# Attention over 128 heads on one core: unrolled engine programs become loops, and the order of the odd halves changes

## The chip, the cores and the metric

The kernel runs on one core of a Trainium2 chip. The time is the device time in microseconds (us); before the change the median of three runs is 635.95 us (635.76 to 636.34). Lower is better. The engines are TensorE (PE), VectorE (DVE), ScalarE (ACT), GpSimd (POOL) and SyncE (SP); SP and ACT issue the transfers (DMA), which run on 16 DMA engines.

## The reference

```
B, H, Sq, Skv, Dh = 8, 16, 16, 2048, 256          # all bf16
scale  = Dh ** -0.5
scores = einsum('bhqd,bhkd->bhqk', q, k) * scale
attn   = softmax(scores, axis=-1)
out    = einsum('bhqk,bhkd->bhqd', attn, v)
```

There are 128 heads with 16 query rows each. K and V have 134 MB each and are read once; Q and the output have 1 MB each.

## The kernel before, in words

The work is cut into 16 rounds g of 8 heads, and each round into two halves e of 4 heads, here called the even (e = 0, or a) and the odd (e = 1, or b) half. One half of K or V is a unit of 4 MiB: 128 partitions, each with 64 tokens of one head (32 partitions a head), 256 numbers a token. `SL` holds four units: KA, KB, VA, VB. The first K units go to VA and VB, so that the K units of round 1 can follow at once.

For each round:

- DVE transposes K in place, in blocks of 32 by 32 and as 32-bit words (four instructions a unit, line 154), and adds one to `c_kt` after each.
- PE multiplies by the queries (lines 234 and 235). `QW` holds Q spread out with zeros so that one product of 128 rows serves 4 heads; 16 products for half a unit, 64 for a round, into the four banks of `S_ps`. After a half is done, `c_qk` goes up, and SP may reuse the K slot.
- DVE takes the row maximum (line 156), ACT the exponential into `P_sb` with the row sums (line 206), DVE transposes it into `PTc` (line 162), and ACT spreads it by eight copies into `PTz` (line 219, four for each half).
- PE multiplies with V, 64 products for each half (line 251). This is done one round late: in the loop's pass g PE first does the score products of round g and then the output products of round g - 1, both halves.
- ACT reads each half out of `O_ps`, divided by the row sum (line 180), and stores 64 KB a round (line 184). It also writes the next round's queries into `QW` (line 174).

Only PE has a loop (line 266), over the rounds 1 to 15; the programs of SP, DVE and ACT are written out for all rounds. In PE's program the last output products, for round 15, stand behind the loop.

SP issues the loads in a fixed order, and each waits there for its slot: Q, K0a, K0b, K1a, K1b, V0a, V0b, and then for each further round K(g)a, K(g)b, V(g-1)a, V(g-1)b. Nothing behind a waiting load is issued. The last V units go to the K slots, and the very last one comes in eight pieces of 19 to 2 tokens, so that the products can follow the landings.

Of the kernel before, what the change touches and what calls it, by code (L numbers as in the profile page):

```python
# [4 lines left out]
ACTF = mybir.ActivationFunctionType  # L5
ALU = mybir.AluOpType
AX = mybir.AxisListType
PE = mybir.EngineType.PE
BF16 = mybir.dt.bfloat16
F32 = mybir.dt.float32  # L10

T = 64
KA, KB, VA, VB = 0, 1, 2, 3


def bass_standalone__softmax_full_bidir__sampling_kernel(
# [17 lines left out]
    qh = q.rearrange("b h s d -> (b h) (s d)")  # L34
    oh = out.rearrange("b h s d -> (b h s) d")

    with ExitStack() as es:
# [5 lines left out]
        PTc = ec(nc.sbuf_tensor("PTc", [128, T, 32], BF16))  # L43
        PTz = ec(nc.sbuf_tensor("PTz", [128, 2, T, 128], BF16))
        O_fin = ec(nc.sbuf_tensor("O_fin", [128, 2, D], BF16))
        negm = ec(nc.sbuf_tensor("negm", [128, G], F32))
        lsum = ec(nc.sbuf_tensor("lsum", [128, G, 2], F32))
        ltot = ec(nc.sbuf_tensor("ltot", [128, G], F32))
        rinv = ec(nc.sbuf_tensor("rinv", [128, G], F32))

        S_ps = ec(nc.psum_tensor("S_ps", [128, 4, 512], F32))
        O_ps = ec(nc.psum_tensor("O_ps", [128, 4, 512], F32))
# [4 lines left out]
        s_q = sem("s_q")  # L57
        s_k = [sem("s_ka"), sem("s_kb")]
        s_k0 = [sem("s_k0a"), sem("s_k0b")]
        s_v = [sem("s_va"), sem("s_vb")]  # L60
        s_st = [sem("s_st%d" % i) for i in range(2)]
# [4 lines left out]
        c_kt = [[sem("c_kt%d%d" % (e, h)) for h in range(2)] for e in range(2)]  # L66
        c_qk = [sem("c_qka"), sem("c_qkb")]
# [5 lines left out]
        c_pv = [sem("c_pv0"), sem("c_pv1")]  # L73
        c_pl = sem("c_pl")
# [4 lines left out]
        def ap_of(t_ap, offset, dims):  # L79
            return bass.AP(tensor=t_ap.tensor, offset=offset, ap=[list(t_ap.ap[0])] + [list(d) for d in dims])  # L80


        TAIL = [(0, 19), (19, 14), (33, 10), (43, 7), (50, 5), (55, 4), (59, 3), (62, 2)]
        TAIL_A = [(0, 37), (37, 27)]
        s_tail = [sem("s_t%d" % i) for i in range(len(TAIL))]
        s_vl = [sem("s_vl%d" % i) for i in range(len(TAIL_A))]
        s_vc = sem("s_vc")
        s_kl = sem("s_kl")

        def obank(g, e):  # L90
            return e + (2 if g == last else 0)

        def kslot(g, e):
            return (VA, VB)[e] if g == 0 else (KA, KB)[e]
# [3 lines left out]

        def on_sync(eng):
            eng.dma_start(QT[:], qh).then_inc(s_q, 16)  # L100
            for e in range(2):
                load(eng, ku, 0, e, kslot(0, e), 0, T, s_k0[e])
            for g in range(1, G):
                for e in range(2):
                    if g >= 2:
                        eng.wait_ge(c_qk[e], g)
                    if (g, e) != (last, 1):
                        load(eng, ku, g, e, kslot(g, e), 0, T, s_k[e])
                    else:
                        load(eng, ku, g, e, kslot(g, e), 0, 32, s_k[e])  # L110
                        load(eng, ku, g, e, kslot(g, e), 32, 32, s_kl)
                w = g - 1
                for e in range(2):
                    if w:
                        eng.wait_ge(c_pv[e], w)
                    else:
                        eng.wait_ge(c_qk[e], 1)
                    if (w, e) != (last - 1, 1):
                        load(eng, vu, w, e, (VA, VB)[e], 0, T, s_v[e])
                        if e:  # L120
                            eng.sem_inc(s_vc, 16)
                    else:
                        load(eng, vu, w, e, VB, 0, 32, s_v[e])
                        load(eng, vu, w, e, VB, 32, 32, s_vc)

            eng.wait_ge(c_qk[0], G)
            for (a, n), s in zip(TAIL_A, s_vl):
                load(eng, vu, last, 0, KA, a, n, s)
            eng.wait_ge(c_qk[1], G)
            for (a, n), s in zip(TAIL, s_tail):  # L130
                load(eng, vu, last, 1, KB, a, n, s)
            eng.wait_ge(c_ev, 2 * last + 2)
            eng.dma_start(oh[128 * last:128 * last + 128, :], O_fin[:, last % 2, :]).then_inc(s_fin, 16)
            eng.wait_ge(s_fin, 16)

        def on_gpsimd(eng):
            eng.memset(PTz[:].rearrange("p a t c -> p (a t c)").bitcast(F32), 0.0).then_inc(c_pool, 1)  # L137

        def on_vector(eng):
            eng.memset(QW[:].rearrange("p e m x -> p (e m x)").bitcast(F32), 0.0).then_inc(c_qt, 1)  # L140
            eng.wait_ge(s_q, 16)
            qf = QT[:].bitcast(F32)
            eng.transpose(qf, qf).then_inc(c_qt, 1)  # L143
            for g in range(G):
                for e in range(2):
                    for c in range(4):
                        if g == 0 and c == 0:
                            eng.wait_ge(s_k0[e], 16)
                        elif c == 0:
                            eng.wait_ge(s_k[e], 16 * g)  # L150
                        elif (g, e, c) == (last, 1, 2):
                            eng.wait_ge(s_kl, 16)
                        x = SLf[:, kslot(g, e), 16 * c:16 * c + 16, :].rearrange("p t i -> p (t i)")
                        eng.transpose(x, x).then_inc(c_kt[e][c // 2], 1)  # L154
                eng.wait_ge(c_qk[1], g + 1)
                eng.tensor_reduce(out=negm[:, g:g + 1], in_=S_ps[:].rearrange("p c n -> p (c n)"),  # L156
                                  axis=AX.X, op=ALU.max, negate=True).then_inc(c_mx, 1)
                for h in range(2):
                    eng.wait_ge(c_ex[h], g + 1)
                    if g and h == 0:  # L160
                        eng.wait_ge(c_cp, 8 * g)
                    eng.transpose(PTc[:, 32 * h:32 * h + 32, :].rearrange("p t x -> p (t x)"),  # L162
                                  P_sb[:, 1024 * h:1024 * h + 1024]).then_inc(c_pt, 1)
                eng.tensor_reduce(out=ltot[:, g:g + 1], in_=lsum[:, g, :], axis=AX.X, op=ALU.add).then_inc(c_ri, 1)  # L164
                eng.wait_ge(c_ri, 2 * g + 1)
                eng.reciprocal(rinv[:, g:g + 1], ltot[:, g:g + 1]).then_inc(c_ri, 1)  # L166

        def on_scalar(eng):
            def qwb(g):
                Q, r = g // 4, g % 4  # L170
                for a in range(4):
                    dv = QW[32 * a:32 * a + 32, 0, 16 * a, :]
                    sv = QT[32 * Q:32 * Q + 32, :]
                    eng.activation(ap_of(dv, dv.offset, [[1024 + 512, 2], [2, 64], [1, 2]]),  # L174
                                   ap_of(sv, sv.offset + 2 * (8 * r + a), [[8, 2], [64, 64], [1, 2]]),
                                   ACTF.Copy, scale=scale).then_inc(c_qw, 1)

            def evac(g, e):
                rows = slice(64 * e, 64 * e + 64)
                eng.activation(O_fin[rows, g % 2, :], O_ps[rows, obank(g, e), 0:D],  # L180
                               ACTF.Copy, scale=rinv[rows, g:g + 1]).then_inc(c_ev, 1)

            def store(g):
                eng.dma_start(oh[128 * g:128 * g + 128, :], O_fin[:, g % 2, :]).then_inc(s_st[g % 2], 16)

            def finish(g):
                eng.wait_ge(c_ri, 2 * g + 2)
                if g >= 2:
                    eng.wait_ge(s_st[g % 2], 16 * (g // 2))
                for e in range(2):  # L190
                    eng.wait_ge(c_pv[e], g + 1)
                    evac(g, e)
                eng.wait_ge(c_ev, 2 * g + 2)
                store(g)
# [3 lines left out]
            for g in range(G):  # L198
                if g < last:
                    eng.wait_ge(c_qk[1], g + 1)  # L200
                    qwb(g + 1)
                eng.wait_ge(c_mx, g + 1)
                if g:
                    eng.wait_ge(c_pt, 2 * g)
                for h in range(2):
                    eng.activation(P_sb[:, 1024 * h:1024 * h + 1024],  # L206
                                   S_ps[:, 2 * h:2 * h + 2, :].rearrange("p c n -> p (c n)"), ACTF.Exp,
                                   bias=negm[:, g:g + 1], scale=1.0, accum_out=lsum[:, g, h:h + 1]).then_inc(c_ex[h], 1)
                if 0 < g < last:
                    finish(g - 1)  # L210
                if g == 0:
                    eng.wait_ge(c_pool, 1)
                eng.wait_ge(c_pt, 2 * g + 2)
                z = 1 if g == last else 0
                for e in range(2):
                    for a in range(4):
                        rs = 32 * (2 * e + a // 2)
                        sv = PTc[rs:rs + 32, :, :]
# [99 lines left out]
```

## Time and profile before

| what | us |
|---|---|
| median of three runs | 635.95 |
| profiled execution: its own time | 636.1 |
| its span, first to last instruction | 634.8 |
| PE busy (products) | 488.3 |
| DVE busy | 365.2 |
| ACT busy | 214.8 |
| DVE waiting for K to land | 157.9 |
| all transfers | 270.64 MB, mean 426 GB/s |

The span was cut into 40 equal slices; a digit is the busy share of a slice in tenths. The chain of waits goes back from the last instruction to what released it, step by step. In the timeline a row has the start, the duration, the engine, the line, the operation and its operands, and in brackets how long the engine was idle before it and what ended that. Rows of SPq are the moments at which SP issues transfers. A row of a window has the busy time of PE, weight loads, DVE, ACT and POOL, the granted clock of TensorE, the share of the DMA engines and their rate in GB/s.

### The profile page before, as it was taken

Reading aid. Unit: us, or ns where it says so; the run is one execution under the profiler, and the core shown is the slowest. Engines: PE = TensorE matmul, PEld = TensorE weight load, DVE = VectorE, ACT = ScalarE, POOL = GpSimd, SP = SyncE. Lnnn points to the kernel's source line nnn. Section 1 sums busy time; section 2 is a strip of 40 time slices with the busy share of each in tenths; the row PEclk is TensorE's granted clock in tenths of the full one; section 3 lists DMA queues with packets and bytes.
Section 4 is the critical chain, followed back from the end, with each engine's and each line's share of the span. In section 5 each row is a group of like instructions: output and inputs, shape, how many; then the busy total and the mean of one; then the engine's idle time right before and its main releaser. Section 6 shows DMA issues by size and latency. Waiting matters only on the chain.

```text
span 634.8 us, 6396 instructions
## 1 busy us (share of the span) xinstructions
PE 488.3 (77%) x3072; PEld 274.9 (43%) x2560; DVE 365.2 (58%) x210; ACT 214.8 (34%) x289; POOL 7.1 (1%) x5
## 2 busy tenths in 40 slices
PE   0738989595896958869597795967959689595998
PEld 0202828154271532716336262452724527144287
DVE  2968583763738546294562945739366393663830
ACT  1042252525035250342513325142252322524170
POOL 4000000000000000000000000000000000000000
PEclk9978999798997989969799797998979989798899
DMA  8999999999999999999999999999999999999997
GB/s 376 436 441 432 428 432 432 430 430 431 432 429 434 429 432 433 429 434 429 433 430 429 432 429 433 430 430 433 434 429 436 433 433 432 432 432 425 430 425 285
DMA packets 13113, 270.64 MB, mean 426 GB/s; under 512 B 1456, under 2 KB 3760, under 8 KB 4400
## 3 DMA queue, kind: packets, MB, share of 16 engines
q1 hardware_dynamic: 10944, 269.55, 98.8%
q10 hardware_dynamic: 2160, 0.98, 0.5%
q8 instruction: 3, 0.05, 0.0%
q14 instruction: 6, 0.05, 0.0%
HBM read 269.48 MB, written 1.05 MB: 426 GB/s over the span
## 4 chain that ended last, share of the span: by engine, by line
DMA 58%; PE 23%; DVE 16%; ACT 2%; issue 0%; SPq 0%
DMA SL<-in_k_dram 58%; DVE SL L154 15%; PE S_ps L234 11%; PE S_ps L235 10%; PE O_ps L251 2%; ACT PTz L219 1%; DVE PTc L162 1%; DVE negm L156 1%; ACT P_sb L206 0%; ACT O_fin L180 0%; SPq L97 0%; SPq L100 0%; DVE rinv L166 0%; DVE ltot L164 0%
## 5 line engine op out<-in xcount | busy, mean ns | idle before, releaser
L154 DVE STREAM_TRANSPOSE SL<-SL 128x2048 f32<-128x2048 f32 x128 | 284.2, 2279 | 157.9 <-DMA SL<-in_k_dram 157.9
L234 PE MATMUL S_ps<-SL,QW 128*128 128x512 bf16 x512 | 214.0, 418 | 143.5 <-DVE SL L154 143.3
L251 PE MATMUL O_ps<-SL,PTz 128*128 128x256 bf16 x2048 | 226.3, 273 | 0.9 <-ACT PTz L219 0.7
L234 PEld LDWEIGHTS S_ps<-SL,QW 128*128 128x128 bf16 x512 | 75.1, 147 | 326.6 <-issue 171.7
L251 PEld LDWEIGHTS O_ps<-SL,PTz 128*128 128x128 bf16 x2048 | 199.8, 98 | 30.9 <-issue 4.5
L235 PE MATMUL S_ps<-SL,QW 128*128 128x512 bf16 x512 | 212.5, 415 | 0.0
L219 ACT ACTIVATE PTz<-PTc 32x1024 bf16<-32x1024 bf16 x128 | 134.9, 1054 | 11.3 <-ACT O_fin L180 5.9
L174 ACT ACTIVATE QW<-QT 32x256 bf16<-32x256 bf16 x64 | 26.8, 419 | 243.3 <-PE S_ps L235 236.2
L156 DVE TENSOR_REDUCE negm<-S_ps 128x1 f32<-128x2048 f32 x16 | 36.7, 2292 | 61.4 <-PE S_ps L235 61.4
L180 ACT ACTIVATE O_fin<-O_ps,rinv 64x256 bf16<-64x256 f32 x32 | 15.0, 468 | 137.6 <-PE O_ps L251 137.5
L162 DVE STREAM_TRANSPOSE PTc<-P_sb 128x1024 bf16<-128x1024 bf16 x32 | 37.9, 1224 | 20.3 <-ACT P_sb L206 20.3
L206 ACT ACTIVATE P_sb<-S_ps,negm 128x1024 bf16<-128x1024 f32 x32 | 35.3, 1109 | 25.5 <-DVE negm L156 25.5
L137 POOL MEMSET PTz<- 128x8192 f32 x1 | 6.9, 6924 | 0.3 <-POOLq L303 0.3
L206 ACT ACTIVATION_READ_ACCUMULATOR P_sb<-S_ps,negm 128x1 f32 x32 | 6.3, 196 | 0.0
L143 DVE STREAM_TRANSPOSE QT<-QT 128x2048 f32<-128x2048 f32 x1 | 2.3, 2312 | 3.7 <-DMA QT<-in_q_dram 3.7
L166 DVE RECIPROCAL rinv<-ltot 128x1 f32<-128x1 f32 x16 | 2.6, 164 | 0.5
L164 DVE TENSOR_REDUCE ltot<-lsum 128x1 f32<-128x2 f32 x16 | 1.8, 112 | 0.0
L174 ACT ACT_TABLE_LOAD x1 | 1.3, 1283 | 0.7 <-PEq L303 0.7
L140 DVE MEMSET QW<- 128x1024 f32 x1 | 0.9, 912 | 1.0 <-PEq L303 1.0
L303 POOL MEMSET const-bfloat16-1.0<- 128x1 bf16 x1 | 0.1, 101 | 0.0
L303 POOL MEMSET const-uint8-127<- 128x1 uint8 x1 | 0.1, 101 | 0.0
L303 POOL MEMSET const-float32-0.0<- 128x1 f32 x1 | 0.1, 98 | 0.2 <-issue 0.2
(1 smaller groups left out, 0.1 us busy)
## 6 DMA issues: line engine op xcount, KB each, us to landing
SL<-in_k_dram SPq DMA_DIRECT2D x31, 4096.0 KB, 25.8
SL<-in_v_dram SPq DMA_DIRECT2D x29, 4096.0 KB, 29.1
SL<-in_k_dram SPq DMA_DIRECT2D x2, 2048.0 KB, 23.7
SL<-in_v_dram SPq DMA_DIRECT2D x2, 2048.0 KB, 29.2
SL<-in_v_dram SPq DMA_DIRECT2D x1, 2368.0 KB, 21.6
SL<-in_v_dram SPq DMA_DIRECT2D x1, 1728.0 KB, 25.4
SL<-in_v_dram SPq DMA_DIRECT2D x1, 1216.0 KB, 20.7
QT<-in_q_dram SPq DMA_DIRECT2D x1, 1024.0 KB, 4.9
```

Source lines behind the costliest of these rows:

```text
L137: eng.memset(PTz[:].rearrange("p a t c -> p (a t c)").bitcast(F32), 0.0).then_inc(c_pool, 1)
L154: eng.transpose(x, x).then_inc(c_kt[e][c // 2], 1)
L156: eng.tensor_reduce(out=negm[:, g:g + 1], in_=S_ps[:].rearrange("p c n -> p (c n)"), axis=AX.X, op=ALU.max, negate=True).then_inc(c_mx, 1)
L162: eng.transpose(PTc[:, 32 * h:32 * h + 32, :].rearrange("p t x -> p (t x)"), P_sb[:, 1024 * h:1024 * h + 1024]).then_inc(c_pt, 1)
L166: eng.reciprocal(rinv[:, g:g + 1], ltot[:, g:g + 1]).then_inc(c_ri, 1)
L174: eng.activation(ap_of(dv, dv.offset, [[1024 + 512, 2], [2, 64], [1, 2]]), ap_of(sv, sv.offset + 2 * (8 * r + a), [[8, 2], [64, 64], [1, 2]]),
L180: eng.activation(O_fin[rows, g % 2, :], O_ps[rows, obank(g, e), 0:D], ACTF.Copy, scale=rinv[rows, g:g + 1]).then_inc(c_ev, 1)
L206: eng.activation(P_sb[:, 1024 * h:1024 * h + 1024], S_ps[:, 2 * h:2 * h + 2, :].rearrange("p c n -> p (c n)"), ACTF.Exp, bias=negm[:, g:g ...
L219: eng.activation(PTz[32 * a:32 * a + 32, z, :, 64 * e + 16 * a:64 * e + 16 * a + 16], sv[:, :, 16 * (a % 2):16 * (a % 2) + 16], ACTF.Copy) ...
L234: return eng.matmul(dst, w, x, start=start, stop=stop)
L235: return eng.add_instruction(mybir.InstMatmult(name=nc.get_next_instruction_name(), engine=PE, start_tensor_calc=start, stop_tensor_calc=stop,
L251: ins = eng.matmul(O_ps[:, bank, 0:D], PTz[:, z, t, :], SL[:, slot, t, :], start=(t == 0), stop=(t == T - 1))
```

## The change: what it does

- SP, DVE and ACT get loops over the rounds, as PE has one. Addresses that depend on the round come from registers, and steps that the first or the last rounds leave out stand in branches. Output products and score products of the rounds stay written out inside PE's loop body. The loop no longer names the slot at which its first instruction is loaded.
- Q lies differently in `QT`, so that a round's queries are picked by a column and not by a group of partitions: the source is walked as 4 blocks (a) of 32 rows (u).
- K0a comes in three transfers: five tokens of the rows 0 to 107, five tokens of the rows 108 to 127, and the other 59 tokens of all rows.
- The score products of round 0 run in a loop over e and four pairs of columns, and wait for a whole unit's transposes, not for half of it. The four banks of `S_ps` are first set to zero by four products with zeros.
- DVE transposes a K unit in two instructions, not four.
- The odd half runs one round later than the even one: in pass r PE does the score products of round r, then the odd output products of round r - 2, then the even ones of round r - 1. Both halves now add up in one bank of `O_ps`, which ACT reads out once for all 128 rows. PE's even products wait for this read-out (`c_ev`).
- ACT in round g: exponential of g, read-out of round g - 2, the four odd copies of round g - 1, the store, then (when P of round g is transposed and the even products of g - 1 are done) the four even copies of g. DVE's transposes of P wait until the odd copies of round g - 1 are done (`c_cp`).
- SP's order follows: after K2a, K2b only V1a; from then on K(j)a, K(j)b, V(j-2)b, V(j-1)a. The last V units stay in VA and VB, in pieces, each released by every 16 products (`c_pv`).
- Semaphores that would have to be waited for at zero start at one or more, added by POOL.

The core of the diff:

```diff
-    qh = q.rearrange("b h s d -> (b h) (s d)")
+    qh = q.rearrange("b h s d -> (b h) (s d)").rearrange("(u a) n -> a u n", a=4)
...
+        def k_and_v(eng, j, es):
+            for e in range(2):
+                eng.wait_ge(c_qk, 8 * j + 4 * e - 4)
+                load(eng, ku, j, e, KA + e, 0, T, s_k[e])
+            for e in es:
+                w = j - 1 - e
+                eng.wait_ge(c_pv, 8 * w + 4 * e + 4)
+                load(eng, vu, w, e, VA + e, 0, T, s_v[e])
...
         def on_sync(eng):
             eng.dma_start(QT[:], qh).then_inc(s_q, 16)
-            for e in range(2):
-                load(eng, ku, 0, e, kslot(0, e), 0, T, s_k0[e])
...
+            for lo, hi in ((0, 108), (108, 128)):
+                eng.dma_start(SL[lo:hi, VA, 0:FEW, :], ku[0, lo:hi, 0:FEW, :]).then_inc(s_k0[0], 16)
+            load(eng, ku, 0, 0, VA, FEW, T - FEW, s_k0[0])
+            load(eng, ku, 0, 1, VB, 0, T, s_k0[1])
...
+            for j in range(2, 3):
+                k_and_v(eng, j, (0,))
+            with nc.Fori(3, last, engines=[SP]) as j:
+                k_and_v(eng, j, (1, 0))
...
         def on_vector(eng):
...
+            with nc.Fori(0, G, engines=[DVE]) as g:
+                eng.wait_ge(c_qk, 8 * g + 8)
+                eng.tensor_reduce(out=negm[:], ...)
                 for h in range(2):
                     eng.wait_ge(c_ex[h], g + 1)
+                    if h == 0:
+                        eng.wait_ge(c_cp, 8 * g + 9)
                     eng.transpose(PTc[...], P_sb[...]).then_inc(c_pt, 1)
...
         def on_scalar(eng):
...
+                with eng.If_ne(g2, 0):
+                    evac(n)
+                with eng.If_ne(gg, 0):
+                    eng.wait_ge(c_pv, 8 * g)
+                    copies(1)
+                with eng.If_ne(g2, 0):
+                    store(n, (g + 14) & 15)
+                eng.wait_ge(c_pt, 2 * g + 2)
+                eng.wait_ge(c_pv, 8 * g + 4)
+                copies(0)
...
         def on_tensor(eng):
...
+            with nc.Fori(0, 2, engines=[PE]) as e:
+                with nc.Fori(0, 4, engines=[PE]) as b:
+                    eng.wait_ge(c_kt, 2 * e + 2)
+                    for par in range(2):
+                        for c in range(4):
+                            ins = mm(S_ps[:, c, :], QW[:, e, :, 2 * b + par], SLk[:, VA + e, c, b, par, :, :], ...)
+                    ins.then_inc(c_qk, 1)
-            with nc.Fori(1, G, engines=[PE], head_slot={PE: 0}) as g:
+            with nc.Fori(1, G + 2, engines=[PE]) as r:
+                with eng.If_lt(rr, G):
...
+                with eng.If_ne(rr, 1):
+                    eng.wait_ge(c_cp, 8 * r + 1)
+                    eng.wait_ge(s_v[1], 16 * (r - 1))
+                    pv(1, ...)
+                with eng.If_lt(rr, G + 1):
+                    eng.wait_ge(c_ev, rr)
+                    eng.wait_ge(c_cp, 8 * r + 5)
+                    eng.wait_ge(s_v[0], 16 * r)
+                    pv(0, ...)
```

290 lines of the change are left out of this document (130 added, 160 removed).

## The prediction

> **What bounds the kernel now.** I read the page first (busy shares, the 40 slices, the DMA queues), then the chain of waits, then the timeline of the opening, of one later round and of the end.
>
> ```profile
> span 634.8 us, 6396 instructions
> PE 488.3 (77%) x3072; PEld 274.9 (43%) x2560; DVE 365.2 (58%) x210; ACT 214.8 (34%) x289; POOL 7.1 (1%) x5
> ...
> DMA  8999999999999999999999999999999999999997
> GB/s 376 436 441 432 428 432 432 430 430 431 432 429 434 429 432 433 429 434 429 433 430 429 432 429 433 430 430 433 434 429 436 433 433 432 432 432 425 430 425 285
> ...
> q1 hardware_dynamic: 10944, 269.55, 98.8%
> ...
> q8 instruction: 3, 0.05, 0.0%
> q14 instruction: 6, 0.05, 0.0%
> ...
> DMA 58%; PE 23%; DVE 16%; ACT 2%; issue 0%; SPq 0%
> ...
> SL<-in_k_dram SPq DMA_DIRECT2D x31, 4096.0 KB, 25.8
> ...
> QT<-in_q_dram SPq DMA_DIRECT2D x1, 1024.0 KB, 4.9
> ```
>
> Every slice but the first and last has the DMA engines 90% busy or more at about 432 GB/s: the kernel is bound by the bytes. A unit of 4 MiB takes 4.194 MB / 432 GB/s = 9.7 us, and lands 25.8 us after its issue (median), so it usually has some 16 us of other loads ahead of it. An engine that gets later by less than that costs nothing; a queue that runs dry costs its whole gap. So I ask two things: does the queue stay filled, and do all 16 DMA engines carry the same bytes?
>
> The opening, where the cushion is thinnest (start, duration, engine, work, idle before):
>
> ```profile
> 0.74 0.38 SPq L100 DMA_DIRECT2D QT<-in_q_dram  x1
> 1.17 2.09 SPq L97 DMA_DIRECT2D SL<-in_k_dram  x4
> 15.34 8.89 DVE L154 STREAM_TRANSPOSE SL<-SL 128x2048 f32<-128x2048 f32 x4 [7.39 <-DMA SL<-in_k_dram]
> 25.05 8.89 DVE L154 STREAM_TRANSPOSE SL<-SL 128x2048 f32<-128x2048 f32 x4 [0.82 <-DMA SL<-in_k_dram]
> 34.28 0.38 PE L235 MATMUL S_ps<-SL,QW 128*128 128x512 bf16 x1
> 34.50 0.38 PE L234 MATMUL S_ps<-SL,QW 128*128 128x512 bf16 x1
> 37.78 2.29 DVE L156 TENSOR_REDUCE negm<-S_ps 128x1 f32<-128x2048 f32 x1 [3.84 <-PE S_ps L235]
> 40.11 1.11 ACT L206 ACTIVATE P_sb<-S_ps,negm 128x1024 bf16<-128x1024 f32 x1 [0.60 <-DVE negm L156]
> 41.34 2.37 DVE L162 STREAM_TRANSPOSE PTc<-P_sb 128x1024 bf16<-128x1024 bf16 x2 [1.27 <-ACT P_sb L206]
> 43.81 8.60 ACT L219 ACTIVATE PTz<-PTc 32x1024 bf16<-32x1024 bf16 x8 [1.41 <-DVE PTc L162]
> 43.87 17.64 DVE L154 STREAM_TRANSPOSE SL<-SL 128x2048 f32<-128x2048 f32 x8
> 56.96 8.70 SPq L97 DMA_DIRECT2D SL<-in_k_dram  x2
> 65.34 2.29 DVE L156 TENSOR_REDUCE negm<-S_ps 128x1 f32<-128x2048 f32 x1 [3.83 <-PE S_ps L235]
> 74.79 8.89 DVE L154 STREAM_TRANSPOSE SL<-SL 128x2048 f32<-128x2048 f32 x4 [3.28 <-DMA SL<-in_k_dram]
> 87.51 10.23 SPq L97 DMA_DIRECT2D SL<-in_k_dram  x2
> ```
>
> I write K2a for the even half of round 2's K, and so on. K0a and K0b land at about 15.3 and 25.05 (DVE waited for both). At 9.7 us a unit, the n-th unit of the queue is done at 25.05 + 9.7(n-2). K2a is the 7th unit: it was issued at 56.96, and the six ahead of it last until 63.9. That is the thinnest place. K3a is the 11th, issued at 87.51 with the ten ahead lasting until 102.7. Data flows some 1.7 us after an issue (an estimate: Q was issued at 0.74 and landed 4.9 us later, of which its bytes at 432 GB/s are 2.4 us; I give most of the rest to the start).
>
> **Part 1, the Q load.** Before, Q is 128 rows of 8 KB. The queue's 10944 packets are its 76 transfers times 144: 128 rows and 16 small ones, one for each DMA engine, so every transfer so far has 8 rows on each of 16 engines. Now Q's source is walked as 4 blocks of 32 rows, so the outermost count is 4. No transfer with such a count is in the trace. The two ends: all 16 engines share it (0 us), or the blocks are dealt out and 4 engines carry 32 rows each. Then those four move 256 KiB at 432/16 = 27 GB/s, 9.7 us in place of 2.4: **7.3 us** later. K0a needs all 16 engines, so it lands 7.3 us late, and with it everything after; and these four engines have 7.3 us more to carry in the whole run, which at 98.8% busy nothing hides. I take the 4-engine end: the transfers in the trace are divided along their outermost dimension, and here that has 4 entries. The Trainium skill's page "DMA: Bandwidth & Descriptors", section "Why a DMA increments its semaphore by 16 and not by 1", says that the engines used are the largest number up to 16 that divides the count of the slowest dimension on both sides: 4 for Q. By that rule 128 rows use 16 engines, which the 10944 packets agree with; no row here shows a count of 4.
>
> **Part 2, the five tokens.** 128 x 2560 B is 0.33 MB, 0.76 us of the whole queue, and no byte is added. Bounds: 0 if evenly spread, +0.3 if the lower engines carry 11 rows for 8 (3 x 2560 B / 27 GB/s), at most 0.76. I take 0.3. Two more issues on SP of 0.4 us hide behind Q's transfer.
>
> **Part 3, the first unit's products.** PE waits for both halves of an even or odd K before its first product: 32 products, not 16, are left when K0b is transposed at 25.05 + 8.89 = 33.94. Their pitch is 0.22 us (34.28 to 34.50), so +16 x 0.22 = 3.5 us. They are now in a loop, with a register instruction for each: 0 to 0.1 us each, 0 to 3.2 us in all; I take 0.5, since PE's present loop shows no such idle time. The row maximum moves from 37.78 to 41.8. K2a is issued 19.2 us behind it (37.78 to 56.96), at 61.0, with data at 62.7: ahead of 63.9, so no gap, but only 1.2 us are left.
>
> **Part 4, the new order of round 1.** Before, DVE transposes the weights P of round 1 right behind the exponential. Now ACT must first make the four odd-half copies of round 0, since these left round 0's ACT work and DVE waits for them. From the maximum at 65.34 + 4.0 = 69.3: 2.3 maximum, 2.3 two exponentials, 4.3 four copies (8.60 / 2), 2.4 P transposes, 0.7 the rest and the loop's branch; K2a's transposes start at 81.3, where before they started at 74.79. K3a is issued when K2a's products are done, 12.7 to 13.1 us on (74.79 to 87.51, 43.87 to 56.96): 94.4, with data at 96.1. And only nine units lie ahead of it now, since V1b has moved behind K3a and K3b on SP; they last until 25.05 + 7 x 9.7 = 93.0. **Gap: 3 us.** Bounds 2 (no loop cost) to 7 (3.2 us in the first loop, 1 in round 1). If the Q load is late, both sides move alike and the gap stays.
>
> **Part 5, all other rounds.**
>
> ```profile
> 97.22 14.16 PE L251 MATMUL O_ps<-SL,PTz 128*128 128x256 bf16 x128
> 97.42 2.29 DVE L156 TENSOR_REDUCE negm<-S_ps 128x1 f32<-128x2048 f32 x1 [3.83 <-PE S_ps L235]
> 104.46 0.47 ACT L180 ACTIVATE O_fin<-O_ps,rinv 64x256 bf16<-64x256 f32 x1 [2.42 <-PE O_ps L251]
> 112.30 8.60 ACT L219 ACTIVATE PTz<-PTc 32x1024 bf16<-32x1024 bf16 x8 [0.41 <-ACT O_fin L180]
> 113.91 8.89 DVE L154 STREAM_TRANSPOSE SL<-SL 128x2048 f32<-128x2048 f32 x4 [10.33 <-DMA SL<-in_k_dram]
> 152.91 8.89 DVE L154 STREAM_TRANSPOSE SL<-SL 128x2048 f32<-128x2048 f32 x4 [10.22 <-DMA SL<-in_k_dram]
> ```
>
> A round is 39.0 us (113.91 to 152.91). In the new one, P's transposes wait for: one half of the output products (7.1), the one read-out (0.5), four copies (4.3); with 2.4 and 0.7 after them K's transposes start 15.0 us behind the last product, where today's start at 16.7 because K isn't there. What hides it is the 10.33 us in which DVE waits for K; some 1.7 are left. With the transposes (17.7) and the last products (3.9) the chain closes in 36.6 us, 2.4 below 39.0: no further gap. PE's new wait for the read-out between its two halves (0.7) lies in its idle time before the next K; the V load queued behind it still has over 10 us of cushion. Fewer, longer transposes save some 0.2 us a round that nobody waits for.
>
> **Part 6, the end.**
>
> ```profile
> 618.53 14.15 PE L251 MATMUL O_ps<-SL,PTz 128*128 128x256 bf16 x128 [0.69 <-ACT PTz L219]
> 632.71 0.47 ACT L180 ACTIVATE O_fin<-O_ps,rinv 64x256 bf16<-64x256 f32 x1 [6.44 <-PE O_ps L251]
> 633.21 0.35 SPq L133 DMA_DIRECT2D out_dram<-O_fin  x1
> 630.00:631.00 1.00, 1.00 (x12) 0.90 (x10) 0.00 (x0) 0.00 (x0) 0.00 (x0) 1.00 0.33 119
> 631.00:632.00 1.00, 1.00 (x12) 0.90 (x10) 0.00 (x0) 0.00 (x0) 0.00 (x0) 1.00 0.04 14
> ```
>
> Today the last 14 us are PE's, released by the copies; the loads end near 631.3 (the last two columns are the DMA share and GB/s), the products at 632.7. Now five V units follow the last K, not four, so PE's backlog is done before the last pieces land, and two tokens (0.2 us) are left then: **-1.0 us**. Fewer instruction blocks are fetched through the same DMA engines (9 packets now): 0 to -1; I take -0.2.
>
> **Sum.** 636.1 (profiled execution; span 634.8 and 1.3 around it) + 7.3 + 0.3 + 3.0 - 1.0 - 0.2 = 645.5. The profiled run stands 0.15 above the median of 635.95. As the unknown loop costs only add (each extra 0.1 us in the opening chain enters the gap in full), I say **646.0**; its own range, from a gap of 2 to one of 7, is 644 to 650.5. A difference of 0.2% is 1.3 us, about what a measurement of this kernel can tell from no change.
>
> **Rivals.**
> *Q is shared by all 16 engines* (0.20). For it: every transfer in the trace is. Then 636.1 + 0.3 + 3.0 - 1.2 = 638.2, with the gap's bounds 637 to 642.
> *The rounds become bound by the DVE chain* (0.06). The margin is 2.4 us a round; if branches, register waits and code loading on ACT, DVE and PE together take 3.4, each of some 14 rounds is 1.0 longer: 645.5 + 14 = 659.5. Against it: PE runs 15 passes of its loop now, with nine instruction packets in the whole run. The skill's page "Runtime: NRT & Kernel Launch", section "Instruction fetch mechanics", warns that a taken branch out of the loaded blocks stalls for a fetch; the trace of PE's loop does not show it for each pass.
> *Not slower: the queue never runs dry* (0.08). If K3a is issued before 91.3, and Q is evenly spread, only the end counts: 636.1 - 1.2 = 634.9. For it: the cushion of 16 us in all later rounds. Against it: the four copies and the 32 products are serial, and 94.4 would have to be wrong by 3 us. It decides at K3a's issue alone. A partial gap gives no change.
> That the 108 and 20 rows do nothing that can be seen is within the 0.3 of part 2 and moves none of these.
>
> **Chances.** 4 engines: 0.66; 16 engines: 0.20; chain-bound: 0.06; not slower: 0.08, of which 0.05 faster and 0.03 within 0.2%. Slower: 0.92. The range 637 to 651 holds the first two cases with their bounds, and leaves out the others.
>
> **What would show it.** Q's issue to landing near 12 us, not 4.9; the first K transposes near 23; a maximum of round 0 near 49; one slice near 95 to 105 us with less than 400 GB/s; no further dip; output products that end within 0.5 us of the last landing. It is wrong if Q still lands in 5 us, if DVE stops waiting for K in the later rounds, or if the slices show no dip.

## The result, and the profile after

The changed kernel takes **663.48 us** (median of five, 662.12 to 663.53), the kernel before 636.01 (five, 635.76 to 636.34): a ratio of 1.0425, 95% interval 1.0411 to 1.0439. The forecast was 646.0 with a range of 637 to 651: slower was right, by how much was not. The profiled execution took 662.12 and is the fastest of the five; its span grew from 634.8 to 660.6, by 25.8. The accounts below are of this execution.

The page of the changed kernel (span, the DMA engines' share and rate in 40 slices, the queues):

```profile
span 660.6 us, 7355 instructions
...
DMA  8999789899999999999999999999999999999997
GB/s 165 253 437 395 319 334 437 345 431 441 421 443 421 441 424 439 433 429 441 421 442 416 445 425 439 433 429 433 426 445 415 446 419 442 431 429 432 418 432 321
...
q1 hardware_dynamic: 11226, 269.55, 97.3%
...
q8 instruction: 1, 0.02, 0.0%
q14 instruction: 1, 0.01, 0.0%
```

The packets of q1 say how many engines each new load used. The prediction counted 144 for a transfer of 128 rows on 16 engines, one small packet for each engine. Here 76 transfers of that kind account for 10944, and 282 packets are left for Q and the two pieces of five tokens: 256 rows and 26 small ones, which fits 4 engines for Q, 12 for the 108 rows and 10 for the 20.

From the ninth slice on the rate is what it was, but for the last slice. All that is lost lies in the first eight slices, 132 us, and the largest part in the first two, where the engines are marked 80 and 90% busy but move 165 and 253 GB/s. The windows of the changed kernel put sizes to that (start:end, busy time of five engines, clock, DMA share, GB/s):

```profile
4.00:28.00 24.00, 0.00 (x0) 0.00 (x0) 0.00 (x0) 0.00 (x0) 4.60 (x1) 1.00 1.04 201
28.00:57.00 29.00, 10.59 (x36) 1.29 (x9) 19.85 (x5) 1.66 (x4) 0.00 (x0) 1.00 0.95 409
77.00:88.00 11.00, 11.00 (x41) 2.98 (x20) 11.00 (x3) 0.00 (x0) 0.00 (x0) 0.79 0.35 125
117.00:121.00 4.00, 4.00 (x19) 1.30 (x9) 4.00 (x2) 0.00 (x0) 0.00 (x0) 1.00 0.54 164
```

Each window's loss is its length times one minus its rate over 432: 24 x (1 - 201/432) = 12.8 us, 1.5, 7.8 and 2.5, together 24.6. The kernel before loses nothing in these stretches. Of the two ends, the first 4 us of the changed kernel lose 1.1 more than before (46 GB/s for 168), and its last slice 1.2 less (15.9 us at 285 GB/s before, 16.5 us at 321 now), which makes 24.5 of the 25.8. A window counts a packet where it starts, so each of these figures is uncertain by some half a microsecond: with each packet spread over its own duration the dip around 117 to 121 comes to 3.1 in place of 2.5. The timeline of DVE and of SP shows which loads these are:

```profile
28.21 2.31 DVE L150 STREAM_TRANSPOSE QT<-QT 128x2048 f32<-128x2048 f32 x1 [26.28 <-DMA QT<-in_q_dram]
38.45 8.77 DVE L154 STREAM_TRANSPOSE SL<-SL 128x4096 f32<-128x4096 f32 x2 [7.93 <-DMA SL<-in_k_dram]
48.18 8.77 DVE L154 STREAM_TRANSPOSE SL<-SL 128x4096 f32<-128x4096 f32 x2 [0.96 <-DMA SL<-in_k_dram]
64.91 2.29 DVE L162 TENSOR_REDUCE negm<-S_ps 128x1 f32<-128x2048 f32 x1 [7.95 <-PE S_ps L249]
85.83 7.37 SPq L96 DMA_DIRECT2D SL<-in_k_dram  x2
92.88 2.29 DVE L162 TENSOR_REDUCE negm<-S_ps 128x1 f32<-128x2048 f32 x1 [4.16 <-PE S_ps L249]
101.84 2.37 DVE L169 STREAM_TRANSPOSE PTc<-P_sb 128x1024 bf16<-128x1024 bf16 x2 [6.67 <-ACT PTz L207]
104.58 17.42 DVE L154 STREAM_TRANSPOSE SL<-SL 128x4096 f32<-128x4096 f32 x4
118.04 8.28 SPq L96 DMA_DIRECT2D SL<-in_k_dram  x2
```

Q lands at 28.2 us, not at 12, and K0a at 38.45, 23.1 later than before (15.34) and not 7.3. The dip at 77 to 88 is the second part of that loss, not a new one: the engines without Q had run ahead into K0b and K1, and have nothing left until K2a is issued at 85.83, while those with Q still carry the rest (from 79 to 85 a window has 109 GB/s at a DMA share of 0.25: four engines). 1.1, 12.8, 1.5 and 7.8 make 23.2, beside the 23.1 by which K0a is late. The small dip at 117 to 121 stands ahead of K3a (issued at 118.04).

### The profile page after: what moved, and what is told of

It is laid out like the page before. It is cut to its first block, busy times and chain, and to the rows that moved or that the text cites. A ratio compares the mean times of both kernels' runs of the same rounds, so it can differ in the third digit from the quotient of the medians.

```text
span 660.6 us, 7355 instructions
## 1 busy us (share of the span) xinstructions
PE 495.8 (75%) x3076; PEld 271.3 (41%) x2545; DVE 361.0 (55%) x146; ACT 209.1 (32%) x277; POOL 7.1 (1%) x5
## 3 DMA queue, kind: packets, MB, share of 16 engines
HBM read 269.48 MB, written 1.05 MB: 410 GB/s over the span
## 4 chain that ended last, share of the span: by engine, by line
DMA 45%; PE 24%; DVE 17%; issue 9%; ACT 3%; ACTq 1%; SPq 0%; DVEq 0%
DMA SL<-in_k_dram 39%; DVE SL L154 15%; PE O_ps L265 9%; PE S_ps L249 8%; PE S_ps L248 8%; DMA SL<-in_v_dram 7%; ACT PTz L207 3%; DVE PTc L169 1%; DVE negm L162 1%; ACTq L212 0%; DVEq L160 0%; ACT P_sb L222 0%; ACT O_fin L200 0%; SPq L96 0%; SPq L111 0%
## 5 line engine op out<-in xcount | busy, mean ns | idle before, releaser
L154 DVE STREAM_TRANSPOSE SL<-SL 128x4096 f32<-128x4096 f32 x64 | 279.9, 4420 | 34.0 <-DMA SL<-in_k_dram 33.8
L248 PE MATMUL S_ps<-SL,QW 128*128 128x512 bf16 (+1 forms) x496 | 210.1, 424 | 115.2 <-DVE SL L154 115.1
L265 PE MATMUL O_ps<-SL,PTz 128*128 128x256 bf16 x2048 | 229.1, 273 | 15.1 <-ACT O_fin L200 12.3
L249 PE MATMUL S_ps<-SL,QW 128*128 128x512 bf16 (+1 forms) x528 | 216.4, 420 | 0.0
L248 PEld LDWEIGHTS S_ps<-SL,QW 128*128 128x128 bf16 (+1 forms) x496 | 72.8, 147 | 305.3 <-issue 180.6
L194 ACT ACTIVATE QW<-QT 32x256 bf16 (+1 forms) x68 | 28.6, 420 | 342.9 <-PE S_ps L249 313.1
L248 PE MATMUL S_ps<-PTz 128*128 128x512 bf16 x1 | 0.6, 609 | 32.3 <-ACT QW L194 32.3
L200 ACT ACTIVATE O_fin<-O_ps,rinv 128x256 f32 (+1 forms) x16 | 7.6, 474 | 50.2 <-PE O_ps L265 50.2
L173 DVE RECIPROCAL rinv<-ltot 128x1 f32 x16 | 2.6, 164 | 2.1
L249 PE MATMUL S_ps<-PTz 128*128 128x512 bf16 x3 | 1.5, 634 | 0.0
## 6 DMA issues: line engine op xcount, KB each, us to landing
SL<-in_v_dram SPq DMA_DIRECT2D x2, 1024.0 KB, 11.1
```

Source lines behind the costliest of these rows:

```text
L154: eng.transpose(x, x).then_inc(c_kt, 1)
L173: eng.reciprocal(rinv[:, bass.ds(g + 1, 1)], ltot[:]).then_inc(c_ri, 1)
L194: eng.activation(dv, sv, ACTF.Copy, scale=scale).then_inc(c_qw, 1)
L200: eng.activation(O_fin[:, n, :], O_ps[:, 0:D], ACTF.Copy, scale=rinv[:, bass.ds(n, 1)]).then_inc(c_ev, 1)
L248: return eng.matmul(dst, w, x, start=start, stop=stop, skip_group_check=not check)
L249: return eng.add_instruction(mybir.InstMatmult(name=nc.get_next_instruction_name(), engine=PE, start_tensor_calc=start, stop_tensor_calc=stop,
```

## The experiments

Each ran beside the kernel before on the same chip. Where no interval is given, the time is that of a single execution, and the landings in its timeline carry the reading. A landing is the moment at which the first instruction that waits for the load starts. All edits are to the changed kernel or, where the name begins with before, to the kernel before. Where a load is cut into several transfers, the wait for it counts them all; that line isn't shown.

### Is it the Q load alone?

**before_q_blocks**: the kernel before, with Q walked as four blocks. The queries then stand in another order.

```diff
-    qh = q.rearrange("b h s d -> (b h) (s d)")
+    qh = q.rearrange("b h s d -> (b h) (s d)").rearrange("(u a) n -> a u n", a=4)
```

> The kernel before with nothing changed but Q's source walk, 4 blocks of 32 rows (the queries come in another order, so the output is permuted; the work is the same). Theory A: Q lands near 28, K0a near 38, and the time is near 636 + 22 = 658. Theory B, the five-token pieces are needed for the slow opening: Q lands near 12.5, K0a near 22.6, time near 643.

Measured: 660.25 us, 24 above the kernel before. The timeline of DVE in this kernel:

```profile
29.90 2.31 DVE L143 STREAM_TRANSPOSE QT<-QT 128x2048 f32<-128x2048 f32 x1 [27.97 <-DMA QT<-in_q_dram]
39.37 8.89 DVE L154 STREAM_TRANSPOSE SL<-SL 128x2048 f32<-128x2048 f32 x4 [7.16 <-DMA SL<-in_k_dram]
```

The page has 10932 packets on q1, 12 fewer than before: Q has 4 small ones in place of 16, so it ran on four engines. One line of the diff explains 24 of the 27 us; no loop, branch or new order is in this kernel.

**k0_whole**: the changed kernel with K0a as one transfer, no pieces of 108 and 20 rows.

> The changed kernel with K0a in one transfer, Q unchanged in 4 blocks. If the pieces of 108 and 20 rows matter by their engines, the time moves by 0.3 us or less for the balance (662 to 664); if they are part of the slow opening, K0a lands well before 38 us and the time falls by several us.

Measured: 662.41; K0a lands at 38.73 (38.45 with the pieces). Beside the slow Q load the pieces don't show.

### Few engines, or the step in the source?

In the walk by blocks neighbouring partitions come from rows 32 KB apart. **before_q_124** has few engines without that step (two transfers of neighbouring rows, 124 = 4 x 31):

```diff
-            eng.dma_start(QT[:], qh).then_inc(s_q, 16)
+            for lo, hi in ((0, 124), (124, 128)):
+                eng.dma_start(QT[lo:hi, :], qh[lo:hi, :]).then_inc(s_q, 16)
```

> The kernel before with Q in its old order, but in transfers of 124 and 4 rows. If engines are dealt out by the largest count up to 16 that divides the rows, 4 engines carry 31 neighbouring rows each. Theory A with few engines as the cause: Q lands near 28, time near 658, as with the 4 blocks. Theory C, the 32 KB step between the rows of a block is the cause: Q lands near 12, time near 643. If all 16 engines share the 124 rows: 636.

Measured: 657.72, with Q and K0a landing as late as with the blocks:

```profile
27.37 2.31 DVE L144 STREAM_TRANSPOSE QT<-QT 128x2048 f32<-128x2048 f32 x1 [25.44 <-DMA QT<-in_q_dram]
36.84 8.89 DVE L155 STREAM_TRANSPOSE SL<-SL 128x2048 f32<-128x2048 f32 x4 [7.17 <-DMA SL<-in_k_dram]
```

The step isn't needed for the slowness. **q_four** has the step without the few engines: the changed kernel with one transfer for each block of 32 rows.

```diff
-            eng.dma_start(QT[:], qh).then_inc(s_q, 16)
+            for a in range(4):
+                eng.dma_start(QT[32 * a:32 * a + 32, :], qh[a]).then_inc(s_q, 16)
```

> The changed kernel with Q loaded in four transfers of 32 rows each (same place of every row, two rows of each transfer on each of 16 DMA engines if they are dealt out by the outermost count). Theory A, the few-engine Q load is what costs the opening: Q lands near 6 us, K0a near 16, the maximum of round 0 starts near 42, and the time is that of the other parts, 636.1 + 0.3 + 3.0 - 1.2 = 638 (637 to 640). Theory B, the five-token pieces or the loops slow the opening: K0a still lands near 38 and the time stays near 663.

Measured: 642.21 (641.54 to 642.82), ratio 1.0095 (1.0078 to 1.0112). Timeline of DVE and SP, then two windows, of q_four:

```profile
7.90 2.31 DVE L151 STREAM_TRANSPOSE QT<-QT 128x2048 f32<-128x2048 f32 x1 [5.97 <-DMA QT<-in_q_dram]
18.58 8.77 DVE L155 STREAM_TRANSPOSE SL<-SL 128x4096 f32<-128x4096 f32 x2 [8.37 <-DMA SL<-in_k_dram]
84.37 17.42 DVE L155 STREAM_TRANSPOSE SL<-SL 128x4096 f32<-128x4096 f32 x4
98.92 7.37 SPq L96 DMA_DIRECT2D SL<-in_k_dram  x2
94.00:98.00 4.00, 4.00 (x19) 1.24 (x9) 4.00 (x2) 0.00 (x0) 0.00 (x0) 0.96 0.36 156
98.00:102.00 4.00, 4.00 (x20) 1.33 (x10) 3.79 (x1) 0.00 (x0) 0.00 (x0) 1.00 0.57 180
```

21 of the 27 us are gone, so the transfer on four engines is the cause. But the 638 that was expected is missed: Q still lands 2.3 us late (7.90 for 5.64) and K0a 3.2, which neither explanation has; and the dip at K3a is plain (98.92; 4.9 us by the two windows).

### What few engines cost alone, and beside K

My 7.3 us stood for four engines that run at 27 GB/s each. **q_alone** holds the K loads of the changed kernel until Q is there, so that the four engines run by themselves:

```diff
             eng.dma_start(QT[:], qh).then_inc(s_q, 16)
+            eng.wait_ge(s_q, 16)
```

> The changed kernel, but SP waits for Q before it issues any K. Theory A1, four engines alone run at 27 GB/s each and only the transfers beside them slow them: Q lands near 12.5 us, K0a near 24, time near 647. Theory A2, the walk in 4 blocks of 32 rows is slow by itself: Q lands near 28, K0a near 39.5, time near 662.

Measured: 656.31, Q at 20.54, K0a at 33.24: between the two expectations. **before_q76_alone** is the kernel before with the same wait and Q in 76 and 52 neighbouring rows (19 rows on each of 4 engines, then 4 on each of 13), **before_q124_alone** the same with 124 and 4:

> The kernel before with Q in transfers of 76 and 52 rows, and K issued only when Q has landed. 76 rows would be 19 on each of 4 DMA engines, 52 rows 4 on each of 13. The four engines then write at rows 0, 19, 38 and 57 onward, never in the same group of four rows modulo 32. Theory P, engines that write into the same group of four partitions modulo 32 share one way into the memory: here none do, a row of 8 KB takes 0.31 us, Q lands near 9.7 us. Theory N, 4 engines are slow as such (0.54 us a row, as in the run with Q alone): Q lands near 15.

> The same with 124 and 4 rows: 31 rows on each of 4 engines, which start at rows 0, 31, 62 and 93, so that two at a time are in the same group of four modulo 32 for most of the way. Theory P: near half rate, Q lands near 19. Theory N: 31 x 0.54 us, also near 19. If neither holds and the 32 KB step between the rows was what slowed the 4 blocks: near 12.5.

Measured: 643.21 with Q at 10.13 and K0a at 22.23 for the 76 rows; 648.80 with Q at 16.06 (19 was expected) and K0a at 28.26 for the 124. Q's landing and a window within its load, of q_alone, of before_q76_alone and of before_q124_alone:

```profile
20.54 2.31 DVE L151 STREAM_TRANSPOSE QT<-QT 128x2048 f32<-128x2048 f32 x1 [18.61 <-DMA QT<-in_q_dram]
8.00:12.00 4.00, 0.00 (x0) 0.00 (x0) 0.00 (x0) 0.00 (x0) 0.60 (x1) 1.00 0.27 66
```

```profile
10.13 2.31 DVE L145 STREAM_TRANSPOSE QT<-QT 128x2048 f32<-128x2048 f32 x1 [8.21 <-DMA QT<-in_q_dram]
5.00:9.00 4.00, 0.00 (x0) 0.00 (x0) 0.00 (x0) 0.00 (x0) 2.65 (x1) 1.00 0.26 109
```

```profile
16.06 2.31 DVE L145 STREAM_TRANSPOSE QT<-QT 128x2048 f32<-128x2048 f32 x1 [14.13 <-DMA QT<-in_q_dram]
4.00:8.00 4.00, 0.00 (x0) 0.00 (x0) 0.00 (x0) 0.00 (x0) 3.65 (x1) 1.00 0.25 78
```

A DMA share of about a quarter says in all three that 4 of 16 engines are at work. With 76 rows they move 109 GB/s, 27 each, the figure of the prediction. With blocks of 32 rows they move little more than half of that (59 to 66 GB/s in the windows from 4 to 16 us), with 31 rows something between (78, then 94 from 8 to 12 us). What differs is where the four write at one moment: 19 partitions apart, 32, or 31.

**before_q76** is the first of the two without the wait, so Q's four engines run beside K0a on the other twelve.

> The kernel before with Q in 76 and 52 neighbouring rows, on four engines that do not get in each other's way (alone they took 309 ns for a row of 8 KB and had Q there at 10.13), now with K0a queued right behind, as in the changed kernel. Theory 'only Q's own rows collide': the four engines have 9.7 us of Q and 9.7 us of K0a, the other twelve start K0a at once; K0a lands near 22 and the run takes 643 (the 7.3 us of the prediction). Theory 'Q's rows and the K rows beside them collide too, each Q row going into a group of partitions that another engine's K rows are filling': Q lands at 14 to 20 and K0a at 25 to 32, 646 to 653. In the changed kernel, where the four also collide with each other, these were 28.2 and 38.5.

Measured: 645.80. Timeline of DVE and a window:

```profile
15.38 2.31 DVE L144 STREAM_TRANSPOSE QT<-QT 128x2048 f32<-128x2048 f32 x1 [13.45 <-DMA QT<-in_q_dram]
24.96 8.89 DVE L155 STREAM_TRANSPOSE SL<-SL 128x2048 f32<-128x2048 f32 x4 [7.27 <-DMA SL<-in_k_dram]
8.00:12.00 4.00, 0.00 (x0) 0.00 (x0) 0.00 (x0) 0.00 (x0) 0.00 (x0) 1.00 0.98 229
```

K0a is 9.6 us late, and Q lands 5 us later than alone. The 7.3 us of the expectation are too many for this division: the 52 rows go to 13 engines, so the four busiest carry 19 + 4 = 23 rows and not 32. Their 15 rows above the usual 8, at 0.31 us a row, make 4.6 us; the other 5 are Q's rows and K's rows hindering each other. The trace's records of single DMA packets show it on both sides. From 5 to 14 us twelve of K's rows of 32 KB are under way at any time, and each takes 2.1 to 2.4 us, for 1.2 once Q has landed; a row of Q takes 0.51 to 0.66 us, and 0.31 alone.

### Which partitions share a way in

If partitions p and p + 32 share one way into the memory, 32 neighbouring rows on all 16 engines reach half of the ways that 128 rows reach, and 64 rows no more than 32. **before_q_4x32** and **before_q_2x64** are the kernel before with Q in four or two transfers of neighbouring rows, in the old order:

```diff
-            eng.dma_start(QT[:], qh).then_inc(s_q, 16)
+            for a in range(0, 128, 32):                      # 64 in before_q_2x64
+                eng.dma_start(QT[a:a + 32, :], qh[a:a + 32, :]).then_inc(s_q, 16)
```

> The kernel before with Q in four transfers of 32 neighbouring rows, so on 16 engines and in the old order of the queries: no 32 KB step in the source, which the four transfers of the changed kernel's order had. Theory 'ways into the memory': 32 partitions reach only half of the ways in, two engines share each, so Q goes at half rate as it did there (2.4 us more and up to 1 us of issues: Q lands near 8, K0a near 18.3) and the time is about 638.7. Rival 'order in the source': only the extra issues are left, Q lands near 6.2, K0a near 16 and the time is 636 to 637.

> The same with two transfers of 64 neighbouring rows, four rows an engine. Theory 'ways into the memory' with a way shared by partitions p and p + 32: 64 partitions reach no more ways than 32 do, and Q lands near 7.8 and K0a near 18 all the same, 638.5. If a way were shared by neighbouring partitions only, 64 rows would reach twice as many as 32, and Q would land near 6 and K0a near 15.7, 636.3.

Measured: 638.13 and 638.17 (before: 635.93). Timeline and a window within the Q load, first of before_q_4x32, then of before_q_2x64:

```profile
7.71 2.31 DVE L144 STREAM_TRANSPOSE QT<-QT 128x2048 f32<-128x2048 f32 x1 [5.78 <-DMA QT<-in_q_dram]
17.38 8.89 DVE L155 STREAM_TRANSPOSE SL<-SL 128x2048 f32<-128x2048 f32 x4 [7.36 <-DMA SL<-in_k_dram]
4.00:6.00 2.00, 0.00 (x0) 0.00 (x0) 0.00 (x0) 0.00 (x0) 2.00 (x1) 1.00 1.05 225
```

```profile
7.92 2.31 DVE L144 STREAM_TRANSPOSE QT<-QT 128x2048 f32<-128x2048 f32 x1 [5.99 <-DMA QT<-in_q_dram]
17.58 8.89 DVE L155 STREAM_TRANSPOSE SL<-SL 128x2048 f32<-128x2048 f32 x4 [7.35 <-DMA SL<-in_k_dram]
4.00:6.00 2.00, 0.00 (x0) 0.00 (x0) 0.00 (x0) 0.00 (x0) 2.00 (x1) 1.00 1.00 217
```

Both go at 217 to 225 GB/s, half of 432, with all engines marked busy. In the packet records a row of Q takes 0.61 and 0.58 us on average, for 0.32 before, so it's the rows that got slower, and not only the extra issues that take time. That is the sharing expected, and it shows that the 2.3 us of q_four come from the 32 rows of each transfer, not from the source's order.

### The pieces of 108 and 20 rows

Once Q is out of the way, K0a lands 10.7 us behind Q in q_four, but 9.7 in before_q_4x32. **q_four_k0_whole** takes q_four's pieces away; **q_four_five128** keeps the five tokens as one transfer of 128 rows.

```diff
-            for lo, hi in ((0, 108), (108, 128)):
+            for lo, hi in ((0, 128),):                       # q_four_five128
```

> The changed kernel with Q in four transfers (K0a 10.7 us behind Q, 642.2), and K0a in one transfer as before. Theory 'the pieces': the five tokens in 108 and 20 rows use few engines and shared ways in, which costs the 1.0 us by which K0a is later behind Q there than in the kernels with one K0a (9.7 us): K0a lands near 17.5 and the time is 641.2. Rival 'Q's rows at a step of 32 KB in the source': the pieces cost nothing, K0a lands near 18.4, 642.1.

> The same with the five tokens as one transfer of all 128 rows, as it stood before the pieces of 108 and 20. Theory 'the pieces': 128 rows are shared evenly by 16 engines, each with a way of its own; K0a lands near 17.6 and the time is 641.2, as with K0a whole. Rival 'any second transfer, or the step in Q's source': K0a stays near 18.4, 642.1.

Measured: 640.78 (ratio 1.0072, 1.0055 to 1.0089) and 641.21 (1.0079, 1.0062 to 1.0095). K0a lands at 17.27 and 17.44, for 18.58 in q_four:

```profile
17.27 8.77 DVE L153 STREAM_TRANSPOSE SL<-SL 128x4096 f32<-128x4096 f32 x2 [7.20 <-DMA SL<-in_k_dram]
```

```profile
17.44 8.77 DVE L155 STREAM_TRANSPOSE SL<-SL 128x4096 f32<-128x4096 f32 x2 [7.42 <-DMA SL<-in_k_dram]
```

The division into 108 and 20 costs 1.1 to 1.3 us, five tokens in a transfer of their own some 0.2. In the total, 1.0 to 1.4 us below q_four, the intervals overlap; the landings carry the finding (q_four_early below, with the pieces too, has K0a at 18.39).

### The gap at K3a

**q_four_early**: q_four, with the four odd copies of round 0 made in round 0 (two lines of ACT's loop), so that round 1's transposes of P don't wait for them.

```diff
-                with eng.If_ne(gg, 0):
+                gh = eng.to_reg(g >> 1)
+                with eng.If_ne(gh, 0):
                     eng.wait_ge(c_pv, 8 * g)
                     copies(1)
...
                 copies(0)
+                with eng.If_lt(gg, 1):
+                    copies(1)
```

> The run with Q in four transfers, and besides the odd-half copies of round 0 are made right behind the even ones in round 0, not behind round 1's exponential. If the gap at K3a (half the usual rate from 94 to 102 us there) comes from these copies, K's transposes of round 2 start some 5.3 us earlier, at 79, K3a is issued at 93.6 with nine units lasting until 96.2, the gap closes, and the time falls from 642.2 to 637.5. If the gap has another cause it stays at 642.

Measured: 638.86 (638.6 to 639.51), ratio 1.0048 (1.0031 to 1.0065), 3.3 us below q_four, where 4.7 were expected. K2's transposes start 5.5 us earlier and K3a is issued at 92.24; the rates on the page show no dip (two rows of its timeline, then the page):

```profile
78.86 17.57 DVE L155 STREAM_TRANSPOSE SL<-SL 128x4096 f32<-128x4096 f32 x4
92.24 8.52 SPq L96 DMA_DIRECT2D SL<-in_k_dram  x2
GB/s 306 426 428 432 419 436 440 432 432 432 432 431 429 429 431 428 432 430 431 440 436 432 436 432 431 430 432 428 432 428 429 434 434 432 434 424 440 416 430 303
```

### The end

**before_tail**: the kernel before, where only the last round's even products start after four copies, not eight (64 columns of weights), so that the products have caught up when the last pieces of V land.

> The kernel before, with only the last round's end changed: the products of the even half (64 columns of weights) start as soon as the four even copies are there, not all eight, so that the products' backlog is gone before the last pieces of V land. If the last 1 us before is TensorE's (products end 1.4 us behind the last landing), the products end 0.3 us behind the last landing and the time is 635.0, 1.0 below the kernel before. Rival: the end is bound by the landing of the last pieces in both, and the time stays at 636.0.

Measured: 635.79 (635.64 to 636.02), ratio 0.9996 (0.9987 to 1.0005): no difference that can be told. The end of its timeline:

```profile
631.64 0.44 PEld L251 LDWEIGHTS O_ps<-SL,PTz 128*128 128x128 bf16 x5 [0.17 <-DMA SL<-in_v_dram]
632.40 0.47 ACT L180 ACTIVATE O_fin<-O_ps,rinv 64x256 bf16<-64x256 f32 x1 [6.90 <-PE O_ps L251]
```

The products now do wait for the landings, and still end at 632.4, only 0.3 earlier than before (632.7).

## Why the prediction was right or wrong

**Part 1, the Q load, is the step that failed**, in size: 7.3 us predicted, 23.1 measured at K0a. Right in it was that four blocks mean four engines: the packets of q1 and the DMA share of a quarter in q_alone show it, so the rule of the Trainium skill's page "DMA: Bandwidth & Descriptors" on which the prediction leaned holds for this shape. Right also was 27 GB/s an engine, as long as the four write to places that don't share a way in and nothing runs beside them (before_q76_alone: 109 GB/s). Wrong was to use this rate for the blocks, and to let K0a wait only for the four engines' extra rows. In the changed kernel a row of Q took 0.74 us on average in the packet records, from 4 to 26 us, not 0.31, and K's rows on the other engines were slowed as well. The table compares the three divisions by their landings, with Q at 5.64 and K0a at 15.34 in the kernel before (in us; the first two lines are runs of that kernel, the third is q_alone and the changed kernel):

| Q's transfers | rows above 8 on the busiest engines, at 0.31 us | Q alone, later by | K0a beside Q, later by | difference |
|---|---|---|---|---|
| 76 and 52 rows | 15: 4.6 | 4.5 | 9.6 | 5.1 |
| 124 and 4 rows | 24: 7.4 | 10.4 | 21.5 | 11.1 |
| 4 blocks of 32 | 24: 7.4 | 14.9 | 23.1 | 8.2 |

By the last line the 23.1 us split so:

- 7.3 for few engines, as predicted;
- 7.6 more because the four blocks share ways with each other, which Q shows alone;
- 8.2 more that appear only beside K.

The parts don't simply add: with 124 rows the four hinder each other less when alone, and K0a is nearly as late all the same. How much each mechanism has of the last two parts in the changed kernel stays open.

What the first window of the changed kernel shows with it is that the twelve engines without Q suffered as well: 201 GB/s for 24 us are 4.8 MB, 1.05 of them Q's, so K came at some 157 GB/s, where twelve engines at 27 would have moved 324. In the packet records twelve of K0a's rows of 59 tokens are under way at a time; between 6 and 26 us none took less than 2.1 us, and most took 1.1 once Q had landed. That it was so in before_q76 too, where the four engines don't share a way with each other, shows that Q on four engines slows K even then.

The Trainium skill has the map: its page "SBUF — State Buffer", section "Door 1: The DMA port swizzle (why `[64,N]` ≈ `[32,N]`)", says that groups of four partitions go to one of 16 ports, that p and p + 32 use the same one, and that rows 0 to 63 so reach 8 ports as rows 0 to 31 do. The 225 and 217 GB/s of 32 and 64 rows agree with it; by it the four blocks of the changed kernel write in pairs to one port (59 to 66 GB/s for 109), and 76 rows in steps of 19 don't. For the hold-up of the twelve other engines the page "DMA: Bandwidth & Descriptors", section "Back-pressure in remote DMA", has a possible reason, told there of transfers between cores: a full port holds up other engines on the path as well. The rates agree with it, but no run here isolates that path: this last step is argued, not shown.

**Part 2, the pieces**: 0.3 predicted with 0.76 as the most; 1.1 to 1.3 where Q doesn't cover it (q_four against its two variants). The packets of q1 fit 12 and 10 engines, as the 0.3 assumed. It was under-sized, probably by the same oversight, though no run separates the engines from the ways in. In the changed kernel Q's load covers it (k0_whole).

**Part 3, the first unit's products**: from K0b's landing to the maximum 12.73 us before (25.05 to 37.78), 16.73 after (48.18 to 64.91): +4.0, as predicted. No gap was forecast at K2a, with a margin of 1.2 us; in q_four the window 63 to 70, about K2a's issue at 65.22, has 379 GB/s, a loss of 0.9 us, so that the margin was used up.

**Part 4, round 1**: K2's transposes start 11.7 us behind the maximum (92.88 to 104.58; 12.0 predicted). K3a is issued 13.5 us on (12.7 to 13.1), 14.6 in q_four. The gap was to be 3 us, with bounds of 2 and 7: 2.5 by the window of the changed kernel (3.1 with the packets spread), 4.9 by the windows of q_four, 3.3 by the difference of q_four and q_four_early in the times, which also shows that the four copies are its cause.

**Part 5, the other rounds**: nothing lost, as predicted. Where the chain catches up, a round takes 36.0 us (row maxima at 125.83, 161.84 and 197.84 in the timeline; 36.6 predicted). Later DVE's rows in the timeline of the changed kernel are 39.0 apart again, by K's landing:

```profile
308.91 2.29 DVE L162 TENSOR_REDUCE negm<-S_ps 128x1 f32<-128x2048 f32 x1 [3.83 <-PE S_ps L249]
325.58 8.77 DVE L154 STREAM_TRANSPOSE SL<-SL 128x4096 f32<-128x4096 f32 x2 [1.96 <-DMA SL<-in_k_dram]
347.92 2.29 DVE L162 TENSOR_REDUCE negm<-S_ps 128x1 f32<-128x2048 f32 x1 [3.84 <-PE S_ps L249]
```

Of the 10.3 us for which DVE waited for K, 2.0 are left, where 1.7 were predicted. The loops fetched two instruction packets instead of nine, and a round of 36.0 us, below the 36.6 of the sum, shows no sign of a stall in each pass.

**Part 6, the end**: -1.0 predicted, and -0.2 for fewer instruction blocks. The size came out, and the reason given for it didn't. In before_tail, where products that keep up with the landings are the only change, they were worth 0.2 to 0.3, within the noise: most of the 1.4 us between the last bytes (631.3) and the last product (632.7) was not TensorE's backlog. The changed kernel itself loses 1.2 less in its last slice than the kernel before, as reckoned above. There the rate falls at once, where before it was down to 119 GB/s at a DMA share of 0.33 from 630 to 631, with a third of the engines still at work. Windows of the changed kernel:

```profile
656.00:657.00 1.00, 1.00 (x11) 0.73 (x9) 0.00 (x0) 0.00 (x0) 0.00 (x0) 1.00 0.94 331
657.00:658.00 1.00, 1.00 (x11) 0.58 (x8) 0.00 (x0) 0.00 (x0) 0.00 (x0) 1.00 0.09 29
```

Why the engines end together now, no run shows; the fewer instruction blocks, put at 0 to -1, may have a part in it. So that the total agrees with the forecast 1.2 is luck as far as the backlog goes.

The sum with the measured terms: 23.1 + 2.5 (or 3.1) - 1.2 = 24.4 to 25.0, beside 25.8 of span; about 1 us stays open. Had Q cost 7.3 us, the other terms as measured would have given 636.1 + 7.3 + 2.5 (or 3.1) - 1.2 = 644.7 to 645.3, close to the forecast. The prediction's own range was added up loosely: 645.5 with a gap of 2 to 7 in place of 3 is 644.5 to 649.5, not 644 to 650.5, which decides nothing here. The rival in which 16 engines share Q was put at 638.2; q_four, where they do, took 642.2, and K0a's landing 3.2 us late, of which that sum had 0.3, is most of the difference.

## What to carry to other kernels

A transfer into the on-chip memory has two divisions: over the DMA engines, by its outermost count, and over the ways into the memory, by the partitions that are written at one moment. Count both for every rearranged load, also for a small one: 1 MB cost 23 us here, far more than the rest of the rewriting. Where a walk by blocks is needed, one transfer for each block brings 20 of the 23 us back; the best of the changed kernels tried is still 0.5% behind the kernel before.

## What the runs showed of the hardware

- The packets of q1 show how many engines a load used: 16 for 128 rows, and for transfers of 64 or 32 rows; 4 for the walk by 4 blocks; 8 in all for 124 and 4 rows; 17 in all for 76 and 52.
- Four engines that write 32 partitions apart moved 59 to 66 GB/s together; 19 apart, 109.
- 16 engines into 32 or into 64 neighbouring partitions moved 217 to 225 GB/s, half of what 128 partitions take (432), while the DMA share stood at 1.0: a busy share says nothing of the rate, so read both lines of the page.
- A load on four engines hinders the loads beside it on engines that carry none of it: K came at some 157 GB/s, half the rate of twelve engines (324), and in before_q76, where the four had ways of their own, K's rows still took 2.1 to 2.4 us for 1.2.
- Splitting 128 rows into 108 and 20 cost more (1.1 to 1.3 us for 0.33 MB) than moving these bytes takes (0.76).
